# TensorE's order prefers groups of products that have been ready for some time, and the planner's durations of products and transposes are corrected: windowed attention with a rational feed-forward layer

## The chip, the cores and the metric

The kernel runs on one core of a Trainium2 chip. The metric is the device time of one execution in microseconds (us); the time of a kernel is the median of its runs.

## The reference

Attention with 8 batches, 8 heads, 576 positions and 64 values per head, in which each position looks at itself and the 63 before it, and then a feed-forward layer on the 4608 tokens (512 to 2048 to 512) with a rational function in place of an activation:

```python
scores = scale * np.matmul(q, k.transpose(0, 1, 3, 2))
mask = (rel >= 0) & (rel < window)                      # window = 64
scores = np.where(mask, scores, -1000000000.0)
scores = scores - np.max(scores, axis=-1, keepdims=True)
attn = np.exp(scores)
attn = attn / (np.sum(attn, axis=-1, keepdims=True) + 1e-09)
attn_out = np.matmul(attn, v)
...
h = x @ w_in                                            # x: 4608 x 512, w_in: 512 x 2048
P = a[0] + a[1] * h + a[2] * h2 + a[3] * h3
Q = 1.0 + np.abs(b[0]) * np.abs(h) + np.abs(b[1]) * h2
g = P / (Q + 1e-6)
return (g @ w_out).astype(np.float32)                   # w_out: 2048 x 512
```

All is float32.

## The kernel before, in words

**Tiles.** The tokens are cut into 12 chunks of 384 (`CH`), the hidden layer into 16 tiles of 128 (`NF`). One hidden tile of one chunk is a *step*. The first two chunks take their steps in halves (chunk 0 tiles 0 to 7, chunk 1 tiles 0 to 7, chunk 1 tiles 8 to 15, chunk 0 tiles 8 to 15), because the second half of the weights is still loaded and split then; from chunk 2 on, a chunk is 16 steps in a row, 192 steps in all. Each float32 matrix is split into a high and a low part (`xh` and `xl`, `wi_h` and `wi_l`, `gh` and `gl`, `wo_h` and `wo_l`), and a product is made of three.

**A step.** `ffn1` issues 12 products of 128x384 into one of two banks, `h_75` and `h_76`, by turns. ScalarE makes a square (`u`), an absolute value (`r`) and a linear form (`num`) from `h`. VectorE makes the denominator (`u<-u,b_sb,r`), and the numerator in two operations that both read `h` (`num<-num,h`, then `num<-num,ab_sb,h`): the bank is free for new products when these are done. ScalarE makes the reciprocal with a logarithm and an exponential (`r<-u`, `r<-r`); VectorE makes `gh` and, in three more operations, `gl`. Three steps later (`LAG`) `ffn2` multiplies them with the output weights: three products of 128x512 into each of the banks `o_72`, `o_73` and `o_74`, which add up over the 16 steps of a chunk. ScalarE copies them out (`ob`) at the end of it.

**A unit.** The attention of one chunk is done in four units, a pair of heads each, so that there is one unit to four steps, three steps ahead of the place where its chunk needs it (`AHEAD`). A unit is, in order: score products into `ps_s`; two VectorE operations that scale and mask them into `sm`; the row maximum (`nmx<-sm`); six exponentials on ScalarE (`sm<-sm,nmx`), which also add up the rows into `sums`; three VectorE operations in `unit_norm` (`sums<-sums`, the reciprocal `rs<-sums` and the *normalisation* `sm<-sm,rs`); six transposes of 128x128 on TensorE (`unit_transpose`), back into `ps_s`; a copy on ScalarE (`pT`); products with the values into `ps_x`, joined with the next unit's score products; and the parts `xh` and `xl` of the result, which is 128 of the 512 rows of `x` of that chunk.

**What sets the order.** The order of each engine's queue is not that of the program's text. A planner (lines 51 to 226) records every call, gives it a duration from a small table (`cost`), and then plays the program through (`plan`): again and again it takes the engine that can start first, and of the operations that are ready on it by then the one that comes first in the text; the end of that operation, plus a margin for the semaphore, is when those that depend on it become ready. The instructions are then issued in the order of the planned starts (`emit`), so that a planned time that is a little off changes the order, and nothing else: on the chip an engine takes its queue in that order and waits where an operand is missing. Groups (`pl.group`) are issued in one piece: the 12 products of an `ffn1`, the three of one output bank, the six transposes of a unit. All planned instructions carry one line in the profile, that of the call in `emit` (L226 before, L228 after).

Of the kernel before, what the change touches and what calls it, by code (L numbers as in the profile page):

```python
# [27 lines left out]
SLOTS = 3  # L28
WARM = 7
FILL = 430  # L30
C1AT = 0, 0, 1, 3
ON_PE = 2
JOIN = 4
# [17 lines left out]
class Planner:  # L51
# [58 lines left out]
    def cost(self, engine, method, out, reads, kw, args):  # L110
        if isinstance(out, Late):
            n = out.size // 4
        else:
            n = 1
            for _, k in out.ap[1:]:
                n *= k
        if engine == "SP":
            parts = 128 if isinstance(out, Late) else (out.ap[0][1] if out.tensor.__class__.__name__ != "DRamTensorHandle" else 0)
            size = mybir.dt.size(out.dtype) * n * (parts or out.ap[0][1])
            return 400, 400, size  # L120
        if engine == "PE":
            if method == "transpose":
                return 109, 270, 0
            if isinstance(args[2], Late):
                n = args[2].size // 4
            else:
                n = 1
                for _, k in args[2].ap[1:]:
                    n *= k
                if args[2].dtype == F32:  # L130
                    return (45, 270, 0) if args[1].ap[0][1] == 64 else (52, 225, 0)
            return n * 0.452, n * 0.452 + 165, 0
        if engine == "ACT":
            if "accum_out" in kw:
                return 343, 450, 0
            f = args[2] if len(args) > 2 else None
            occ = 58 + 0.813 * n
            if n == 512:
                occ = 640 if method == "copy" and getattr(out, "dtype", None) == F16 else 510
            for k in ("scale", "bias"):  # L140
                if isinstance(kw.get(k), bass.AP):
                    occ += 92
            if f in (AF.Ln, AF.Exp):
                occ += 55
            return occ, occ + 120, 0
        if engine == "DVE":
            if method == "tensor_reduce":
                n = 1
                for _, k in reads[0].ap[1:]:
                    n *= k  # L150
            if n < 16:
                return 90, 185, 0
            occ = 65 + 1.045 * n
            if isinstance(kw.get("scalar"), bass.AP):
                occ += 62
            return occ, occ + 85, 0
        if engine == "POOL":
            return (n * 2.0 + 60, n * 2.0 + 100, 0) if method in ("tensor_scalar", "tensor_copy") else (n * 2.4 + 130, n * 2.4 + 170, 0)
# [24 lines left out]
    def plan(self):  # L183
        waiting = {e: [] for e in self.free}
        missing = [len(o.before) for o in self.ops]
        for o in self.ops:
            if not o.before:
                waiting[o.engine].append(o)
        dma_free = 0
        for _ in self.ops:  # L190
            start, engine = min((max(self.free[e], min(o.ready for o in w)), e) for e, w in waiting.items() if w)
            op = min((o for o in waiting[engine] if o.ready <= start), key=lambda o: o.index)
            waiting[engine].remove(op)
            op.start, self.free[engine] = start, start + op.occ
            op.end = start + op.own + 45
            if engine == "PE":
                op.end = self.free[engine] + 200
            if engine == "SP":
                dma_free = max(dma_free, start + 750) + op.dma / (300 if start < 8000 else 390)
                op.end = dma_free + 1550  # L200
            for o in op.after:
                o.ready = max(o.ready, self.free[engine] if engine == o.engine == "SP" and self.lanes_apart(op, o) else op.end)
                missing[o.index] -= 1
                if not missing[o.index]:
                    waiting[o.engine].append(o)
# [42 lines left out]
def swa_rational_ffn(ctx: ExitStack, tc: tile.TileContext, qk, v, w_in, w_out, out):  # L248
# [107 lines left out]
    pl = Planner(nc, dict(DVE=4700, ACT=2100, PE=WARM * 430 + 1200, POOL=5000, SP=750), shares)  # L356
# [49 lines left out]
    def two_banks(c, hp, transposed):  # L406
        if c == 0 and transposed:
            return [ps_o[0], ps_o[1]], None
        if c == 0 and hp % 2:
            return [h_ring(), h_ring()], None  # L410
        return [ps_s[:, 0], ps_s[:, 1]], ps_s
# [63 lines left out]
    def unit_transpose(c, hp):  # L475
        u = live[c, hp]
        ps, both = two_banks(c, hp, True)
        with pl.group():
            for j in range(2 * PR):
                pl.tensor.transpose(ps[j // PR][:, (j % PR) * P:(j % PR + 1) * P], u["sm"][:, j, :], ident)  # L480
        pT = u["pT"] = pT_ring()
        if both is not None:
            pl.scalar.copy(out=pT, in_=both[:, :, 0:PR * P])
        else:
            for z in range(2):
                pl.scalar.copy(out=pT[:, z], in_=ps[z][:, 0:PR * P])
# [115 lines left out]
    for c, i0, i1 in phases:  # L602
        if c not in seen:
            seen.add(c)
            places += [(C1AT[k] if c == 1 else s - prev + prev // HP * k - AHEAD, c, k, s - prev if c > 1 else 0) for k in range(HP)]
        prev = i1 - i0
        s += prev
    for n, (p, c, k, free) in enumerate(places):
        joined = n >= HP + JOIN
        if joined:  # L610
            p = max(p, places[n - 1][3])
        at(p, unit_load, c, k)
        if joined:
            at(p, av_and_scores, *places[n - 1][1:3], c, k)
        else:
            at(p, unit_scores, c, k)
        at(p, unit_soft, c, k)
        at(p, unit_norm, c, k)
        at(p + 1, unit_transpose, c, k)
        if n + 1 < HP + JOIN or n + 1 == len(places):  # L620
            at(max(p + 1, free), unit_av, c, k)
# [9 lines left out]
    for k in range(HP):  # L631
        unit_scores(0, k)
        unit_soft(0, k)
        unit_norm(0, k)
        unit_transpose(0, k)
        unit_av(0, k)
# [14 lines left out]
    pl.plan()  # L651
    pl.fill("PE", ps_o[2].tensor.name, FILL, (nc.tensor.matmul, (ps_o[2], warm[:, 0:P], warm), dict(start=True, stop=True)))
    pl.emit()
# [37 lines left out]
```

## Time and profile before

| | |
|---|---|
| median of 3 runs | 982.49 us (981.6 to 982.84) |
| the profiled execution | 982.07 us, of which the span from the first to the last instruction is 980.3 |
| TensorE (PE), products / weight loads | 952.6 us (97% of the span) / 824.6 (84%) |
| VectorE (DVE) | 911.2 us (93%) |
| ScalarE (ACT) | 698.5 us (71%) |
| GpSimd (POOL) | 4.4 us (0%) |
| SyncE's transfers | 68.38 MB, 70 GB/s over the span |
| TensorE's granted clock | 0.997 of full speed |

How to read it: a busy share is a mean over stages that differ. In this kernel there are four. Up to about 150 us the weights are loaded and split while the first two chunks run; then both halves of the weights are there; from about 275 us on the chunks 2 to 11 run with one unit of attention to four steps; and at the end, from 881 us, only the last chunk's feed-forward is left. Numbers by stretch say more than the head of the page. A row of a timeline has the start and the duration in us, the engine, the operation, output and operands, and in brackets the idle time ahead of it with what ended it. The ends of TensorE's products are modelled, so a product that is shown with 0.40 us may have its successor start 0.24 us after its own start; what TensorE lost at some place is read from start to start.

### The profile page before, as it was taken

How to read it: one execution, taken by the hardware profiler on the slowest of the kernel's cores; microseconds unless marked ns; L12 is line 12 of the kernel's file. 1: busy time of each engine (PE TensorE's matmuls, PEld its weight loads, DVE VectorE, ACT ScalarE, POOL GpSimd, SP SyncE). 2: the span in 40 equal slices, each digit the busy share in tenths (PEclk: the TensorE clock that was granted, in tenths of full speed). 3: DMA queues.
4: the chain of work that ended last, by engine and by line, in shares of the span. 5: the costliest groups of instructions: out<-in, count | busy, mean ns of one | idle time of the engine just before them, and what ended most of it. 6: DMA issues, size and time to landing. Idle time of an engine off the chain costs nothing.

```text
span 980.3 us, 17701 instructions
## 1 busy us (share of the span) xinstructions
PE 952.6 (97%) x6672; PEld 824.6 (84%) x6675; DVE 911.2 (93%) x1747; ACT 698.5 (71%) x1737; POOL 4.4 (0%) x20
## 2 busy tenths in 40 slices
PE   8899999999999999999999999999999999999998
PEld 5677788888888888888888888888888888888996
DVE  6999999998999999999999999999999899999996
ACT  7988777776667667767677677667766776676664
POOL 1000000000000000000000000000000000000000
PEclk9999999999999999999999999999999999999999
DMA  9344341313103103103102200210310310300000
GB/s 360 127 171 147 122 150 39 96 50 117 51 1 117 35 17 118 35 17 116 37 17 74 79 17 26 93 51 1 118 35 17 118 35 18 100 1 2 33 1 32
DMA packets 24564, 68.38 MB, mean 70 GB/s; under 512 B 2720, under 2 KB 2720, under 8 KB 24480
## 3 DMA queue, kind: packets, MB, share of 16 engines
q1 hardware_dynamic: 24480, 67.27, 20.2%
q8 instruction: 52, 0.85, 0.4%
q14 instruction: 32, 0.26, 0.1%
HBM read 57.03 MB, written 10.22 MB: 69 GB/s over the span
## 4 chain that ended last, share of the span: by engine, by line
PE 64%; DVE 19%; ACT 10%; issue 2%; DMA 1%; ACTq 0%; DVEq 0%
PE o L226 29%; PE h L226 28%; DVE u L226 6%; PE ps_s L226 5%; ACT sm L226 4%; DVE num L226 3%; PE ps_x L226 3%; ACT r L226 2%; DVE gh L226 2%; DVE sm L226 2%; DVE nmx L226 1%; ACT u L226 1%; DVE gl L226 1%; DMA w_st<-w_out 1%; ACT num L226 1%
## 5 line engine op out<-in xcount | busy, mean ns | idle before, releaser
L226 PE MATMUL h<-xl,wi_h 128*128 128x384 f32 x768 | 260.4, 339 | 7.7 <-DVE num L226 6.2
L226 PE MATMUL h<-xh,wi_l 128*128 128x384 f32 x768 | 258.1, 336 | 0.0
L226 PE MATMUL h<-xh,wi_h 128*128 128x384 f32 x768 | 257.9, 336 | 0.0
L226 PE MATMUL o<-wo_h,gl 128*128 128x512 f32 x576 | 236.5, 411 | 2.5 <-DVE gl L226 1.7
L226 PE MATMUL o<-wo_h,gh 128*128 128x512 f32 x576 | 228.2, 396 | 0.0
L226 PE MATMUL o<-wo_l,gh 128*128 128x512 f32 x576 | 227.0, 394 | 0.0
L226 ACT ACTIVATE u<-h 128x384 f32<-128x384 f32 x192 | 94.2, 491 | 158.4 <-PE h L226 153.6
L226 PEld LDWEIGHTS h<-xl,wi_h 128*128 128x128 f32 x768 | 144.2, 188 | 20.3 <-DVE num L226 10.2
L226 PEld LDWEIGHTS h<-xh,wi_h 128*128 128x128 f32 x768 | 144.2, 188 | 7.2
L226 ACT ACTIVATE num<-h,ab_sb 128x384 f32<-128x384 f32 x192 | 129.7, 675 | 25.7 <-PE h L226 15.6
L226 PEld LDWEIGHTS h<-xh,wi_l 128*128 128x128 f32 x768 | 144.2, 188 | 0.3 <-DVE wi_l L226 0.3
L226 ACT ACTIVATE r<-u 128x384 f32<-128x384 f32 x192 | 101.3, 527 | 48.1 <-DVE u L226 44.8
L226 PEld LDWEIGHTS o<-wo_h,gl 128*128 128x128 f32 x576 | 108.1, 188 | 29.0 <-issue 5.1
L226 PEld LDWEIGHTS o<-wo_h,gh 128*128 128x128 f32 x576 | 108.5, 188 | 26.3
L226 DVE SCALAR_TENSOR_TENSOR gh<-num,ab_sb,r 128x384 fp32r<-128x384 f32 x192 | 117.9, 614 | 8.7 <-ACT r L226 1.6
L226 PEld LDWEIGHTS o<-wo_l,gh 128*128 128x128 f32 x576 | 108.7, 189 | 16.5
L226 DVE SCALAR_TENSOR_TENSOR num<-num,ab_sb,h 128x384 f32<-128x384 f32 x192 | 117.3, 611 | 5.6 <-ACT r L226 1.5
L226 DVE SCALAR_TENSOR_TENSOR u<-u,b_sb,r 128x384 f32<-128x384 f32 x192 | 117.9, 614 | 2.9 <-ACT r L226 1.0
L226 DVE SCALAR_TENSOR_TENSOR u<-num,ab_sb,u 128x384 f32<-128x384 f32 x192 | 118.1, 615 | 2.7
L226 ACT ACTIVATE r<-h,ab_sb 128x384 f32<-128x384 f32 x192 | 111.4, 580 | 11.1 <-DVE num L226 11.1
L226 DVE SCALAR_TENSOR_TENSOR u<-u,gh 128x384 f32<-128x384 f32 x192 | 106.4, 554 | 2.7
L226 DVE TENSOR_TENSOR num<-num,h 128x384 f32<-128x384 f32 x192 | 105.0, 549 | 3.5 <-ACT r L226 2.2
(74 smaller groups left out, 983.6 us busy)
## 6 DMA issues: line engine op xcount, KB each, us to landing
qk<-qk SPq DMA_DIRECT2D x44, 419.0 KB, 4.2
vt<-v SPq DMA_DIRECT2D x44, 384.0 KB, 3.6
out<-ob SPq DMA_DIRECT2D x33, 256.0 KB, 2.1
w_st<-w_out SPq DMA_DIRECT2D x15, 512.0 KB, 3.5
w_st<-w_in SPq DMA_DIRECT2D x11, 512.0 KB, 3.6
early<-qk SPq DMA_DIRECT2D x4, 419.0 KB, 5.5
early<-v SPq DMA_DIRECT2D x4, 384.0 KB, 8.1
early_wi_l<-w_in SPq DMA_DIRECT2D x3, 512.0 KB, 9.4
```

Source lines behind the costliest of these rows:

```text
L226: call(*[value(x) for x in args], **{k: value(x) for k, x in kw.items()})
```

## The change

Three edits, all in the planner's input. `MARGIN` gives TensorE 300 ns: of the operations that are ready on it, `plan` first looks among those that were ready at least 300 ns before the start, takes the first of these in the text, and only if there is none takes the first of all that are ready. A column of a product costs 0.4545 ns in place of 0.452, so a product of 384 columns 174.5 ns for 173.6, and one of 512 232.7 for 231.4. A group of six transposes holds TensorE 50 ns longer (6 x 109 + 50 = 704 for 654).

```diff
+MARGIN = dict(PE=300)
...
-            return n * 0.452, n * 0.452 + 165, 0
+            return n * 0.4545, n * 0.4545 + 165, 0
...
             start, engine = min((max(self.free[e], min(o.ready for o in w)), e) for e, w in waiting.items() if w)
-            op = min((o for o in waiting[engine] if o.ready <= start), key=lambda o: o.index)
+            able = [o for o in waiting[engine] if o.ready <= start]
+            op = min([o for o in able if o.ready <= start - MARGIN.get(engine, 0)] or able, key=lambda o: o.index)
...
     def unit_transpose(c, hp):
         u = live[c, hp]
         ps, both = two_banks(c, hp, True)
-        with pl.group():
+        with pl.group(50):
             for j in range(2 * PR):
```

No instruction is added or taken away on any engine. What changes is the order on TensorE, VectorE and ScalarE, first at about 30 us and then all through the program; SyncE's transfers keep theirs. Three places show it.

TensorE, at the transposes of a unit within a chunk, before:

```order
L226 MATMUL o_72<-wo_h_1133,gl_190 128x512
L226 MATMUL o_72<-wo_l_1146,gh_186 128x512
L226 MATMUL o_72<-wo_h_1133,gh_186 128x512
L226 MATMUL ps_s<-ident,sm_172 128x128 x6
L226 MATMUL o_73<-wo_h_1133,gl_190 128x512
L226 MATMUL o_73<-wo_l_1146,gh_186 128x512
```

and now:

```order
L228 MATMUL o_72<-wo_h_1133,gl_190 128x512
L228 MATMUL o_72<-wo_l_1146,gh_186 128x512
L228 MATMUL o_72<-wo_h_1133,gh_186 128x512
L228 MATMUL o_73<-wo_h_1133,gl_190 128x512
L228 MATMUL o_73<-wo_l_1146,gh_186 128x512
L228 MATMUL o_73<-wo_h_1133,gh_186 128x512
L228 MATMUL ps_s<-ident,sm_172 128x128 x6
```

The transposes stand behind two output banks (six products) where they stood behind one (three).

VectorE, from a unit's maximum to its normalisation and on, before:

```order
L226 TENSOR_REDUCE nmx_175<-sm_172 128x6
L226 SCALAR_TENSOR_TENSOR u_183<-num_185,ab_sb,u_183 128x384
L226 SCALAR_TENSOR_TENSOR u_182<-u_182,b_sb,r_180 128x384
L226 TENSOR_TENSOR gl_191<-u_183,r_181 128x384
L226 TENSOR_TENSOR num_184<-num_184,h_75 128x384
L226 SCALAR_TENSOR_TENSOR num_184<-num_184,ab_sb,h_75 128x384
L226 TENSOR_SCALAR sums_177<-sums_177 128x6
L226 RECIPROCAL rs_179<-sums_177 128x6
L226 TENSOR_TENSOR sm_172<-sm_172,rs_179 128x768
```

and now:

```order
L228 TENSOR_REDUCE nmx_175<-sm_172 128x6
L228 SCALAR_TENSOR_TENSOR u_183<-num_185,ab_sb,u_183 128x384
L228 SCALAR_TENSOR_TENSOR u_182<-u_182,b_sb,r_180 128x384
L228 TENSOR_TENSOR gl_191<-u_183,r_181 128x384
L228 TENSOR_SCALAR sums_177<-sums_177 128x6
L228 RECIPROCAL rs_179<-sums_177 128x6
L228 TENSOR_TENSOR sm_172<-sm_172,rs_179 128x768
L228 TENSOR_TENSOR num_184<-num_184,h_75 128x384
L228 SCALAR_TENSOR_TENSOR num_184<-num_184,ab_sb,h_75 128x384
```

The two numerator operations on `num_184`, which stood between the maximum and the operation on `sums`, stand behind the normalisation.

ScalarE in the same unit, before:

```order
L226 ACTIVATE u_182<-h_75 128x384
L226 ACTIVATE r_180<-h_75,ab_sb 128x384
L226 ACTIVATE num_184<-h_75,ab_sb 128x384
L226 ACTIVATE sm_172,sums_177<-sm_172,nmx_175 128x128 x6
L226 ACTIVATE r_180<-u_182 128x384
```

and now:

```order
L228 ACTIVATE u_182<-h_75 128x384
L228 ACTIVATE r_180<-h_75,ab_sb 128x384
L228 ACTIVATE sm_172,sums_177<-sm_172,nmx_175 128x128 x6
L228 ACTIVATE num_184<-h_75,ab_sb 128x384
L228 ACTIVATE r_180<-u_182 128x384
```

The linear form `num_184` stands behind the six exponentials, not ahead of them.

## The prediction

> **What bounds the kernel now.** I read the page's head first, then the busy times by stretch, then the waits, and last the timelines of single engines around the softmax.
>
> ```profile
> span 980.3 us, 17701 instructions
> PE 952.6 (97%) x6672; PEld 824.6 (84%) x6675; DVE 911.2 (93%) x1747; ACT 698.5 (71%) x1737; POOL 4.4 (0%) x20
> ```
>
> The head makes TensorE the bound: 97% against 93% for VectorE. By stretch (the columns are those of the first line):
>
> ```profile
> core 0: us, PE busy (x) PEld busy (x) DVE busy (x) ACT busy (x) POOL busy (x), PEclk, DMA share, GB/s
> 275.40:881.10 605.70, 601.82 (x4277) 529.02 (x4276) 565.81 (x1084) 427.06 (x1078) 0.00 (x0) 1.00 0.16 52
> 151.80:275.40 123.60, 120.48 (x930) 103.97 (x929) 115.39 (x225) 87.17 (x234) 0.00 (x0) 1.00 0.22 70
> 881.10:980.30 99.20, 94.67 (x489) 83.90 (x487) 87.41 (x157) 58.50 (x115) 0.00 (x0) 0.99 0.04 17
> 24.00:140.00 116.00, 103.78 (x704) 84.98 (x704) 115.15 (x223) 100.62 (x226) 0.00 (x0) 1.00 0.44 149
> ```
>
> From 24 to 140 us, while the weights are split, VectorE is busy 115.15 of 116 us: TensorE's order can't shorten that. From 275.4 to 881.1 us TensorE idles 3.9 us and VectorE 39.9 us. What VectorE waits for there decides (view of the waits in that stretch; us in total, times, longest):
>
> ```profile
> DVE sums L226 <- ACT sm L226: 23.1, 31, 1.2
> PE ps_s L226 <- ACT ob L226: 2.7, 4, 0.7
> PE ps_s L226 <- DVE sm L226: 1.2, 4, 0.3
> DVE gh L226 <- PE h L226: 1.5, 10, 0.2
> DVE num L226 <- ACT u L226: 1.3, 4, 0.3
> ```
>
> 23.1 us in 31 waits are for the score exponentials, which VectorE itself released by its maximum. For TensorE it waits 1.5 us in all. So over these 606 us VectorE is a second full engine: it goes round its own loop, normalisation to normalisation, and TensorE waits for it at the transposes. One such loop with its two halves, then the next (VectorE timeline):
>
> ```profile
> 314.41 0.96 DVE L226 TENSOR_TENSOR sm<-sm,rs 128x768 f32<-128x768 f32 x1
> 330.21 0.95 DVE L226 TENSOR_REDUCE nmx<-sm 128x6 f32<-128x768 f32 x1
> 332.60 0.55 DVE L226 TENSOR_TENSOR num<-num,h 128x384 f32<-128x384 f32 x1
> 333.19 0.61 DVE L226 SCALAR_TENSOR_TENSOR num<-num,ab_sb,h 128x384 f32<-128x384 f32 x1
> 334.02 0.17 DVE L226 TENSOR_SCALAR sums<-sums 128x6 f32<-128x6 f32 x1 [0.21 <-ACT sm L226]
> 334.45 0.96 DVE L226 TENSOR_TENSOR sm<-sm,rs 128x768 f32<-128x768 f32 x1
> 349.10 0.95 DVE L226 TENSOR_REDUCE nmx<-sm 128x6 f32<-128x768 f32 x1
> 352.81 0.17 DVE L226 TENSOR_SCALAR sums<-sums 128x6 f32<-128x6 f32 x1 [1.21 <-ACT sm L226]
> 353.24 0.96 DVE L226 TENSOR_TENSOR sm<-sm,rs 128x768 f32<-128x768 f32 x1
> ```
>
> The first loop takes 20.04 us (314.41 to 334.45): 15.80 to the maximum, then 4.24 in which two numerator products fill the wait, so that only 0.21 us are idle. The second takes 18.79: those two products are already done, so the maximum comes after 14.65, and then 4.14 with 1.21 us idle. The pair is 38.83 us. A third kind of loop stands at the chunk boundary:
>
> ```profile
> 294.24 0.96 DVE L226 TENSOR_TENSOR sm<-sm,rs 128x768 f32<-128x768 f32 x1
> 310.23 0.95 DVE L226 TENSOR_REDUCE nmx<-sm 128x6 f32<-128x768 f32 x1
> 295.34 0.85 PE L226 MATMUL ps_s<-ident,sm 128*128 128x128 f32 x6 [0.68 <-ACT ob L226]
> ```
>
> It takes 20.17 (294.24 to 314.41). The transposes at 295.34 start 0.14 after the normalisation ends (294.24 + 0.96), so it is that which they wait for, whatever name the row gives.
>
> The Trainium skill ("Perfetto Trace Analysis", Identifying the Most-Contended Engine) says that matmul busy time does not tell how near TensorE is to its limit, that the share of weight loads does, and that for VectorE occupancy is fair. In this stretch that is 87% (529.02 of 605.70) against 93% (565.81), so by the rule VectorE is the engine to spare. By the 99% of the matmul column the change should pay as in the second rival below; by the rule it should not. The waits above agree with the rule.
>
> **The change part by part.** The new costs, 0.4545 for 0.452 ns a column and 50 ns for a group of transposes, issue nothing; with the margin of 300 ns they only move instructions. No instruction is added or removed on any engine, and SyncE's DMAs keep their order.
>
> (1) The stretch of 31 loops from the normalisation at 275.45 to the last at 881.14.
>
> ```profile
> 275.45 0.96 DVE L226 TENSOR_TENSOR sm<-sm,rs 128x768 f32<-128x768 f32 x1
> 881.14 0.96 DVE L226 TENSOR_TENSOR sm<-sm,rs 128x768 f32<-128x768 f32 x1
> ```
>
> 605.69 us, 19.54 each. In the new order transposes stand behind six output products wherever three or six stood before, and every chunk has the same pattern: one boundary loop (VectorE's order in it is that of 294.24 to 314.41) and three loops in VectorE's order from 314.41 to its maximum. But the two numerator products that filled the wait in about half of the loops now always stand behind the normalisation, because ScalarE's `num` has moved behind the exponentials. So each of the three is 15.80 plus a wait without filling. That is 8 boundary loops and 23 others.
>
> Does 15.80 hold when TensorE is elsewhere? In the stretch VectorE's waits for TensorE are 1.5 us in 10 places; what else holds it between normalisation and maximum are its own results and ScalarE's, which wait for VectorE. So yes.
>
> The second half is 4.14 at most (349.10 to 353.24). It can be shorter, if the exponentials start as soon as the maximum ends:
>
> ```profile
> 349.90 0.58 ACT L226 ACTIVATE r<-h,ab_sb 128x384 f32<-128x384 f32 x1
> 350.36 0.40 ACT L226 ACTIVATE sm<-sm,nmx 128x128 f32<-128x128 f32 x1
> ```
>
> The maximum ends at 350.05, the first exponential starts at 350.36, behind an operation on `h_75`. With 0.05 us for the hand-over that leaves 0.26: lower bound 3.88. TensorE's `h_75` products will stand earlier against VectorE than now, since TensorE is held at the transposes, so I take a value below the middle, 3.95. A loop is then 19.75 (19.68 to 19.94).
>
> Sum: 8 x 20.17 + 23 x 19.75 = 161.4 + 454.3 = 615.6, against 605.7: **+9.9 us** (+8.3 to +14.3). As a cross-check by waits: 31 waits of 0.95 to 1.21 make 29.5 to 37.5 us in place of 23.1, +6.4 to +14.4.
>
> What TensorE gains lies inside this. Where transposes stood behind three output products they waited 0.14:
>
> ```profile
> 353.97 0.40 PE L226 MATMUL o<-wo_h,gh 128*128 128x512 f32 x1
> 354.34 0.84 PE L226 MATMUL ps_s<-ident,sm 128*128 128x128 f32 x6
> 355.26 0.40 PE L226 MATMUL o<-wo_l,gh 128*128 128x512 f32 x1
> 355.50 0.40 PE L226 MATMUL o<-wo_h,gh 128*128 128x512 f32 x1
> ```
>
> Products start 0.24 apart (355.26, 355.50), the transposes 0.37 after the product ahead. That 0.14 (normalisation at 353.24 done at 354.20) goes, and comes back at the boundary: TensorE's work ahead of those transposes is what it was, the loop ahead of them is longer. There nothing else can be issued: the next output products wait for the eviction of the chunk, and `h_75` for its bank.
>
> (2) The stretch 151.8 to 275.4. Transposes that waited for the normalisation move behind a group of `h` or output products there too (the view of waits has them with 2.0 us), and TensorE idles 3.1 us in all (123.60 - 120.48). Lower bound -3.1. Against it: the last two loops here took 35.91 (239.54 to 275.45) and are now of the kinds 18.79 and 19.75: +2.6. Between these I take **-0.5**, about the middle.
>
> ```profile
> PE ps_s L226 <- DVE sm L226: 2.0, 2, 1.0
> 239.54 0.96 DVE L226 TENSOR_TENSOR sm<-sm,rs 128x768 f32<-128x768 f32 x1
> ```
>
> (3) Up to 140 us VectorE is full and has the same instructions to do: 0. If it should find idle time there, it costs what it idles.
>
> (4) After the last normalisation TensorE alone sets the end (94.67 busy of 99.2). The last transposes now have six output products ahead of them, not three: 3 x 0.24 = **-0.7 us** left to do.
>
> Together +9.9 - 0.5 - 0.7 = +8.7 (+4.5 to +16.2). The profiled execution took 982.07 us (its span and 1.8 around it); it becomes 990.8. The median of the runs stands 0.4 above it: **991 us**, 986.6 to 998.5 if this mechanism holds.
>
> **The rivals.** *The boundary wait replaces the others and nothing else changes.* TensorE's waits at the transposes of one boundary, and of the next unit that waits long (its timeline):
>
> ```profile
> 294.33 0.34 PE L226 MATMUL h<-xh,wi_l 128*128 128x384 f32 x1
> 393.46 0.40 PE L226 MATMUL o<-wo_h,gh 128*128 128x512 f32 x1
> 394.15 0.63 PE L226 MATMUL ps_s<-ident,sm 128*128 128x128 f32 x4 [0.29 <-DVE sm L226]
> ```
>
> Against 0.17 from an `h` product to the next start (three quarters of 0.24 for its columns), 294.33 to 295.34 loses 0.84; against 0.23, 393.46 to 394.15 loses 0.46. With three of 0.14 that is 1.72 us in two chunks (156.4 us), while one boundary wait of 0.84 in each chunk is 1.68. Then the time is 982.5 - 0.5 - 0.7 = 981.3; the margin would be measured on the planner's clock and reach nothing on the chip. For it: the pattern at the boundary is the old one. Against it: VectorE's filling is gone, and its loop has no other room. 0.12.
>
> *The transposes stop waiting and TensorE is the bound*, faster. The mechanism: VectorE's 39.9 us idle in the stretch is slack, the normalisation keeps its place in time, and with six products ahead TensorE meets every one done. Price: 1.72 per 156.4 over 605.7 is 6.7, and 1.5 of the 3.1 in the stretch ahead: 982.5 - 6.7 - 1.5 - 0.7 = 973.6. It decides if a loop without filling takes under 19.3 us, which is TensorE's own work for one: (156.4 - 1.72) / 8. For it: the 97%. Against it: no loop with these operations took under 19.68 by its parts. 0.08.
>
> **How the numbers follow.** The forecast has 0.80. A measurement of this kernel tells about 0.2% (2 us) from no change. Of the 0.80 I put 0.02 within that; the first rival is at its edge and gives 0.08 to the same and 0.04 to faster; the second 0.08 to faster. Slower 0.78, same 0.10, faster 0.12. The range leaves out the second rival, most of the first and the last end of the forecast: 982.5 to 997.5.
>
> **What would show it.** VectorE's wait for the exponentials ahead of `sums` (23.1 us, 31 times in the stretch) goes to 30 to 37 with no wait of 0.2 left; loops of 19.7 to 19.9 and 20.2, four to a chunk of 79.2 to 80 us, in place of 78.2; transposes at the boundary wait 1.5 to 2 us in every chunk, and TensorE's busy time stays at 952 us while its share falls to 96%. Wrong would be: loops of 19.4 (then the fixed 15.80 was not fixed), or transposes that never wait with VectorE's idle time unchanged (the second rival).

## The result and the profile after

The changed kernel takes 989.36 us (median of 6 runs, 989.01 to 990.44), the kernel before 982.62 in the same 6 rounds (981.6 to 982.99). The ratio is 1.0072, with a 95% interval from 1.0059 to 1.0085: slower by 6.7 us. The forecast was 991, range 982.5 to 997.5.

The head of the page after shows little of it: TensorE has the same work in a longer span.

```profile
span 987.7 us, 17709 instructions
PE 952.1 (96%) x6675; PEld 828.0 (84%) x6675; DVE 909.0 (92%) x1747; ACT 700.5 (71%) x1737; POOL 4.3 (0%) x20
```

Busy times of the changed kernel from the normalisation at 275.12 to the last at 889.10 (31 loops, the same piece of work as 275.45 to 881.14 before), after it to the end, and in the stretch where the weights are split:

```profile
core 0: us, PE busy (x) PEld busy (x) DVE busy (x) ACT busy (x) POOL busy (x), PEclk, DMA share, GB/s
275.10:889.10 614.00, 601.65 (x4280) 530.86 (x4279) 565.24 (x1085) 429.28 (x1079) 0.00 (x0) 1.00 0.16 52
889.10:987.70 98.60, 94.13 (x487) 83.64 (x485) 87.57 (x156) 58.66 (x115) 0.00 (x0) 1.00 0.04 17
24.00:140.00 116.00, 104.27 (x695) 86.52 (x695) 113.03 (x219) 97.86 (x220) 0.00 (x0) 0.97 0.44 149
```

The 31 loops take 614.0 us where they took 605.7: +8.3. What lies ahead of them is 0.3 shorter (275.12 for 275.45), what lies behind them 0.6 (98.60 for 980.3 - 881.14 = 99.16). That is 7.4 us, the difference of the two profiled executions (989.50 and 982.07).

The waits in that stretch (in total, times, longest):

```profile
DVE sums L228 <- ACT sm L228: 32.0, 31, 1.2
PE ps_s L228 <- ACT ob L228: 12.3, 8, 1.6
```

VectorE's wait for the exponentials is 32.0 us in 31 waits, 23.1 before; all 31 are now full waits, none under 0.96. Its idle time in the loops grew from 39.9 to 48.8 us (614.00 - 565.24), by the same 8.9. TensorE's waits at the transposes, 3.9 us before, are 12.3, in eight places, one to a chunk. Two loops on VectorE's timeline, the boundary's and the one behind it:

```profile
294.79 0.96 DVE L228 TENSOR_TENSOR sm<-sm,rs 128x768 f32<-128x768 f32 x1
310.79 0.94 DVE L228 TENSOR_REDUCE nmx<-sm 128x6 f32<-128x768 f32 x1
314.54 0.17 DVE L228 TENSOR_SCALAR sums<-sums 128x6 f32<-128x6 f32 x1 [1.21 <-ACT sm L228]
314.97 0.96 DVE L228 TENSOR_TENSOR sm<-sm,rs 128x768 f32<-128x768 f32 x1
330.78 0.95 DVE L228 TENSOR_REDUCE nmx<-sm 128x6 f32<-128x768 f32 x1
334.22 0.17 DVE L228 TENSOR_SCALAR sums<-sums 128x6 f32<-128x6 f32 x1 [0.97 <-ACT sm L228]
334.65 0.96 DVE L228 TENSOR_TENSOR sm<-sm,rs 128x768 f32<-128x768 f32 x1
```

20.18 (16.00 and 4.18) and 19.68 (15.81 and 3.87). Every chunk has one loop of the first kind and three of the second, to a hundredth or two (one loop, of 19.73, is longer). TensorE at a boundary, 373.20 to 375.11:

```profile
373.20 0.34 PE L228 MATMUL h<-xh,wi_l 128*128 128x384 f32 x1
375.11 0.85 PE L228 MATMUL ps_s<-ident,sm 128*128 128x128 f32 x6 [1.57 <-ACT ob L228]
```

1.91 us from start to start, where two products of this kind lie 0.17 apart: 1.74 lost. At the first boundary of the stretch it is 1.54, at the others 1.73 to 1.74.

### The profile page after: what moved, and what is told of

It is laid out like the page before. It is cut to its first block, busy times and chain, and to the rows that moved or that the text cites. A ratio compares the mean times of both kernels' runs of the same rounds, so it can differ in the third digit from the quotient of the medians.

```text
span 987.7 us, 17709 instructions
## 1 busy us (share of the span) xinstructions
PE 952.1 (96%) x6675; PEld 828.0 (84%) x6675; DVE 909.0 (92%) x1747; ACT 700.5 (71%) x1737; POOL 4.3 (0%) x20
## 4 chain that ended last, share of the span: by engine, by line
DVE 42%; PE 34%; ACT 18%; issue 4%; DMA 1%; SPq 0%; ACTq 0%; DVEq 0%
PE o L228 16%; PE h L228 14%; DVE u L228 12%; DVE num L228 10%; ACT sm L228 8%; DVE gh L228 7%; ACT r L228 5%; DVE sm L228 3%; DVE gl L228 3%; DVE nmx L228 3%; PE ps_s L228 3%; ACT u L228 2%; DVE xl L228 1%; PE ps_x L228 1%; DVE w_c L228 1%
```

## The experiments

Two theories. **A, the filling**: VectorE's loop sets the pace, and the change costs time because the two numerator operations no longer fill the wait between maximum and `sums`. **B, the transposes**: they stand behind six products instead of three, come later, and hold back the unit's chain (copy, value products, scores, maximum); the order on VectorE is only a sign of it.

The table gives the median with its ratio to the kernel before of the same runs, and from the profiled execution: the time to the normalisation at which the 31 loops start, their length, what lies behind the last (to the end of the span), and VectorE's waits for the exponentials within the loops.

| kernel | median us | ratio (95%) | to the loops | 31 loops | behind | waits |
|---|---|---|---|---|---|---|
| before | 982.6 | | 275.45 | 605.69 | 99.16 | 23.1 |
| the change | 989.4 | 1.0072 (1.0059 to 1.0085) | 275.12 | 613.98 | 98.60 | 32.0 |
| margin alone | 978.2 | 0.9968 (0.9955 to 0.9980) | 272.65 | 605.18 | 98.47 | 20.6 |
| column cost alone | 987.9 | 1.0062 (1.0048 to 1.0076) | 271.84 | 614.09 | 99.17 | 32.0 |
| change without the column cost | 982.1 | 1.0005 (0.9996 to 1.0014) | 277.09 | 604.55 | 98.56 | 21.8 |
| change, filled by hand | 990.7 | 1.0095 (1.0081 to 1.0109) | 279.05 | 611.01 | 98.44 | 5.2 |
| the same, boundary transposes later | 987.3 | 1.0059 (1.0047 to 1.0072) | 279.75 | 606.40 | 98.45 | 5.3 |
| before, filling taken away by hand | 993.3 | 1.0118 (1.0103 to 1.0133) | 276.61 | 617.80 | 99.09 | 30.1 |
| change, exponential at 390 ns | 973.3 | 0.9909 (0.9896 to 0.9923) | 273.55 | 599.24 | 98.41 | 16.6 |
| the same, filling taken away by hand | 988.1 | 1.0068 (1.0055 to 1.0080) | 277.04 | 611.03 | 98.93 | 29.5 |
| change, exponential at 390 ns, without the margin | 972.5 | 0.9910 (0.9897 to 0.9924) | 272.63 | 599.60 | 98.47 | 16.6 |
| before, exponential at 390 ns | 979.0 | 0.9977 (0.9968 to 0.9986) | 276.35 | 601.83 | 98.62 | 19.0 |
| 0.449 ns, margin, exponential at 390 | 977.4 | 0.9949 (0.9935 to 0.9962) | 275.81 | 602.28 | 98.21 | 13.8 |
| margin 600, exponential at 390 | 986.6 | 1.0055 (1.0042 to 1.0067) | 277.65 | 609.37 | 96.98 | 11.9 |

Counted in the traces, the two numerator operations stand between the maximum and `sums` in 16 of the 32 units of this piece before, in none of the change and of the column cost alone, and in 16 with the margin alone and in the change without the column cost. They do so in 4 units (before) and 8 (exponential at 390 ns) where the filling was taken away by hand, in 24 in the change with the exponential at 390 ns, with and without the margin, and in the kernel before with it, and in all 32 in the two rows filled by hand and the last two of the table. From none over 16 to 24 filled units the loops get shorter (614, 605, 599 to 602 us); with all 32 filled they take 602 to 611, for reasons given below.

### The parts of the change apart

Margin alone:

```diff
 MARGIN = dict(PE=300)
-            return n * 0.4545, n * 0.4545 + 165, 0
+            return n * 0.452, n * 0.452 + 165, 0
-        with pl.group(50):
+        with pl.group():
```

> The margin of 300 ns alone, with the costs of the kernel before (0.452 ns a column, no 50 ns for the transposes). The transposes within a chunk stand behind six output products (or nine or twelve), but about half of the units keep the two numerator operations in the wait. Theory A: the mean loop stays near 19.5, and TensorE's small waits of 0.14 go: 981 to 983 us. Theory B: the transposes are as late as in the changed kernel: 987 to 990.

Column cost alone:

```diff
-MARGIN = dict(PE=300)
+MARGIN = dict(PE=0)
             return n * 0.4545, n * 0.4545 + 165, 0
-        with pl.group(50):
+        with pl.group():
```

> 0.4545 ns a column alone, no margin and no 50 ns. The transposes stand behind three output products in every unit within a chunk, but no unit has the two numerator operations in the wait. Theory A: loops of 19.67 and 20.18 as in the changed kernel, 989 to 990.5 us, and waits at the transposes behind three products of 0.3 to 0.5 us that cost nothing further. Theory B: transposes earlier than in the changed kernel, so the time of before or less: 980 to 983.

The change without its column cost:

```diff
 MARGIN = dict(PE=300)
-            return n * 0.4545, n * 0.4545 + 165, 0
+            return n * 0.452, n * 0.452 + 165, 0
         with pl.group(50):
```

> The change without its column cost (0.452 ns as before): the margin of 300 ns and the 50 ns for the transposes stay. Half of the units keep the two numerator operations in the wait. Theory A: mean loop 19.52 as with the margin alone, 977 to 981 us, so that the column cost alone carries the loss. If the 50 ns carry part of the loss: 984 us or more.

The 31 loops by busy times (columns as above) and their waits, first of the margin alone, then of the column cost alone:

```profile
272.65:877.83 605.18, 601.64 (x4280) 530.49 (x4280) 567.26 (x1087) 427.69 (x1081) 0.00 (x0) 1.00 0.16 52
```

```profile
DVE sums L228 <- ACT sm L228: 20.6, 19, 1.2
```

```profile
271.84:885.93 614.09, 604.22 (x4280) 529.18 (x4279) 565.36 (x1085) 431.69 (x1080) 0.00 (x0) 1.00 0.16 52
```

```profile
DVE sums L228 <- ACT sm L228: 32.0, 31, 1.2
PE ps_s L228 <- DVE sm L228: 2.8, 15, 0.2
```

The column cost alone brings the whole loss of the 31 loops: 614.09 against 613.98 of the change, with the same 32.0 us of waits, although its transposes stand behind three products (15 of them wait for the normalisation, 0.2 each in this view, 0.33 to 0.38 from start to start). The margin alone moves the transposes behind six or nine products within a chunk and loses nothing there: 605.18 against 605.69. Theory B is out as a cause of the +8.3. In time, taking the column cost out of the change makes it 982.1, the time of before.

Both runs with a single part left their forecast on the good side (978.2 against 981 to 983; 987.9 against 989 to 990.5), by what happens ahead of the loops: 2.8 and 3.6 us less than before; margin and 50 ns together have 1.6 more, outside the 977 to 981 that was expected. These 272 to 277 us move with the order in a way that no run here takes apart.

### The filling given back, and taken away

The planner was left as it is, and after it had set the order three operations of a unit were moved in the queues of ScalarE and VectorE, TensorE's order untouched. In the changed kernel, in 34 of 36 units:

```diff
     pl.plan()
+    pl.move_fill(True)
...
+            if into:
+                nums = [o for o in act if o.start > last.start and writes(o) == "num"][:1]
...
+            new = (first.start - 0.01, sums.start - 0.02, sums.start - 0.01) if into else (max(num.start, last.start + 0.01), norm.start + 0.01, norm.start + 0.02)
...
+                num.start, n1.start, n2.start = new
```

> The changed kernel with its TensorE order untouched. In the 34 units where it can be done, ScalarE's linear form num is issued ahead of the six exponentials instead of behind them, and VectorE's two numerator operations ahead of the operation on sums instead of behind the normalisation. Theory A (the filling of VectorE's wait is what was lost): the second half of a loop is 4.14 to 4.24 us with a wait of about 0.2 in place of 3.87 with 0.97, the first 14.65 in place of 15.80; a loop of 18.9 is under TensorE's own 19.34, TensorE becomes the bound, and 31 loops save 31 x (19.81 - 19.34) = 14.6 us against the changed kernel: 975 us, at most 980 if TensorE still loses time at the boundary. Theory B (the transposes behind six products come too late and hold back the unit's chain, the order on VectorE is only a sign of it): the first half of the loop stays at 15.8 less the two operations plus a wait for TensorE, time 988 to 990.

In the kernel before, `pl.move_fill(False)`, which moves the same three operations behind the exponentials and the normalisation in 13 units:

> The kernel before with its TensorE order untouched (transposes behind three, six and twelve products). In 13 of the 17 or so units of chunks 1 to 11 whose wait is filled, num goes behind the exponentials and the two numerator operations behind the normalisation (in four units it can't be done, since the bank would be read too late). Theory A: about 15 loops of 19.7, 8 boundary loops of 20.17 and 8 loops that still make pairs of 38.83, sum 612 in place of 605.7: 989 us. Theory B: TensorE's transposes stand where they stood, so 982.6, at most 984.

The kernel before without the filling loses 12.1 us in the 31 loops (617.80), with 30.1 us of waits. That is theory A's sign and about twice its size (+6.3 was expected). The expectation left eight loops in pairs of 38.83, but no loop of 18.79 is left: 19.87 stands in their place. The first two loops are together another 2.8 longer (41.72 for 38.96). The four loops in which only two operations are left between maximum and `sums`, with a wait of 1.5, take 19.76 as they did before. TensorE waits at the transposes too, 12.3 us in the two rows below where it waited 3.9, so this run does not show the filling alone:

```profile
DVE sums L255 <- ACT sm L255: 30.1, 31, 1.5
PE ps_s L255 <- ACT ob L255: 6.2, 4, 1.9
PE ps_s L255 <- DVE sm L255: 6.1, 7, 1.1
```

The changed kernel with the filling given back is *not* faster, 990.7 where 975 to 980 was expected. Its loops:

```profile
298.40 0.96 DVE L257 TENSOR_TENSOR sm<-sm,rs 128x768 f32<-128x768 f32 x1
318.71 0.17 DVE L257 TENSOR_SCALAR sums<-sums 128x6 f32<-128x6 f32 x1 [0.65 <-ACT sm L257]
319.14 0.96 DVE L257 TENSOR_TENSOR sm<-sm,rs 128x768 f32<-128x768 f32 x1
338.06 0.17 DVE L257 TENSOR_SCALAR sums<-sums 128x6 f32<-128x6 f32 x1
338.50 0.96 DVE L257 TENSOR_TENSOR sm<-sm,rs 128x768 f32<-128x768 f32 x1
```

Within a chunk the loop does what theory A says: 19.36 (319.14 to 338.50), no wait ahead of `sums`, TensorE's own 19.34. But the boundary's loop went from 20.18 to 20.74, so that a chunk saves only 0.4 us and the loops 3.0 in all (23 that are 0.32 shorter, 8 that are 0.56 longer). The time ahead of the loops grew by 3.9, where two units were moved too, and one of these accounts for nearly all of it:

```profile
206.29 0.55 DVE L257 TENSOR_TENSOR num<-num,h 128x384 f32<-128x384 f32 x1 [4.75 <-ACT u L257]
```

ScalarE's `num`, put ahead of this unit's exponentials, starts at 202.89 after 4.74 us of idle time for TensorE's products, and the exponentials stand behind it; VectorE then idles 4.75 us. From the normalisation ahead to this unit's is 14.95 us (192.88 to 207.83), 11.12 in the changed kernel. So a good part of the 990.7 comes from where one unit was put by hand, ahead of the loops, and not from the filling in them.

What holds the boundary is TensorE's wait at the transposes:

```profile
297.93 0.34 PE L257 MATMUL h<-xh,wi_l 128*128 128x384 f32 x1
299.50 0.85 PE L257 MATMUL ps_s<-ident,sm 128*128 128x128 f32 x6 [1.24 <-DVE sm L257]
```

1.57 from start to start, 1.40 lost, where no other unit waits. In the order of the change the boundary's transposes stand two output banks (6 x 0.235 = 1.4 us of products) nearer to those ahead of them than a regular unit's, since the banks that could go first are not copied out yet: VectorE would have to make one loop in four 1.4 us shorter than the rest. So a second cause stands beside the filling. To test it, the same kernel with these transposes put behind the first output bank of the new chunk:

```diff
+            o, late = queue[k], queue[k + 1]
+            if kind(queue[k - 1]) == "h" and kind(late).startswith("o"):
+                t = late.start + 0.01
+                if all(q.start > t for q in o.after):
+                    o.start = t
```

> The changed kernel with every unit filled by hand (990.7 us, in-chunk loops 19.35, boundary loops 20.74 with a TensorE wait of 1.40), and with the transposes of the boundary unit moved behind the first output bank of the new chunk (three products), so that TensorE's work between them and the transposes ahead is 17.9 us in place of 17.2. If the boundary wait comes from where those transposes stand: it halves, a chunk goes from 78.8 to about 78.1 us, 984 to 987. If it comes from the unit's chain on VectorE and ScalarE: 990 to 991.

```profile
298.63 0.34 PE L268 MATMUL h<-xh,wi_l 128*128 128x384 f32 x1
299.57 0.50 PE L268 MATMUL o<-wo_h,gl 128*128 128x512 f32 x1 [0.60 <-ACT ob L268]
300.37 0.82 PE L268 MATMUL ps_s<-ident,sm 128*128 128x128 f32 x6
```

TensorE now waits for the copy of the bank (0.94 from start to start, 0.77 lost) and not for the normalisation. The loops take 606.4 in place of 611.0, a chunk 78.2 in place of 78.8, the median 987.3: the saving per chunk was right, the time 0.3 above the forecast since the start was another 0.7 later. (From start to start, TensorE's work ahead of these transposes is 17.94 us without the move and 18.74 with it, not 17.2 and 17.9; the step is the one expected.) So the boundary transposes' place cost 0.6 us a chunk in this order.

### The planner's missing cost

The rows of ScalarE show what the planner had not been told. In the changed kernel, the maximum on VectorE's timeline, and then ScalarE's, with the first three of a unit's exponentials, which add up their rows:

```profile
350.46 0.94 DVE L228 TENSOR_REDUCE nmx<-sm 128x6 f32<-128x768 f32 x1
```

```profile
350.28 0.58 ACT L228 ACTIVATE r<-h,ab_sb 128x384 f32<-128x384 f32 x1
351.44 0.40 ACT L228 ACTIVATE sm<-sm,nmx 128x128 f32<-128x128 f32 x1 [0.58 <-DVE nmx L228]
351.84 0.39 ACT L228 ACTIVATE sm<-sm,nmx 128x128 f32<-128x128 f32 x1
352.22 0.39 ACT L228 ACTIVATE sm<-sm,nmx 128x128 f32<-128x128 f32 x1
```

They start 0.38 to 0.40 us apart; the planner's table has 343 ns. Corrected as well:

```diff
             if "accum_out" in kw:
-                return 343, 450, 0
+                return 390, 497, 0
```

> The changed kernel with one more cost corrected: an exponential that adds up its row is charged 390 ns of ScalarE in the planner, which is its spacing in the trace (351.84, 352.22, 352.61, ... in the changed kernel: 0.385 us), in place of 343. The planner then puts num ahead of the exponentials and the two numerator operations into the wait again, in three units of four, and the transposes go behind nine output products in two of four. Theory A: in-chunk loops of 19.35, boundary loops of 20.2, stretch 8 x 20.2 + 23 x 19.4 = 608, against 614 in the changed kernel: 981 to 985 us. Theory B (late transposes cost): the transposes are later still, 989 us or more.

```profile
273.55:872.79 599.24, 599.24 (x4281) 532.13 (x4280) 566.45 (x1087) 425.46 (x1081) 0.00 (x0) 1.00 0.16 53
```

```profile
DVE sums L228 <- ACT sm L228: 16.6, 23, 1.2
```

973.3 us, faster than before by 0.9% and better than forecast (981 to 985). In the 31 loops TensorE has no idle time that the records show: 599.24 busy in 599.24 us, 19.33 a loop, and no wait at any transposes, the boundary's included. The forecast had 20.2 for a chunk's boundary loop and 19.4 for each of its others; in fact the four loops of a chunk are 20.36, 19.34, 18.83 and 18.78 us, together 77.3, which is four times 19.33, so the boundary costs nothing extra here. The Trainium skill's rule on load share ("Perfetto Trace Analysis", Identifying the Most-Contended Engine) would still name VectorE here, 95% (566.45 of 599.24) against 89% (532.13); the measurement does not agree, since here it is TensorE that never waits.

Is it the filling, or the transposes, which now stand behind nine products in half of the units? The same kernel with `pl.move_fill(False)`, which empties two of the three filled units of a chunk and leaves TensorE's order:

> The run with the exponential at 390 ns, its TensorE order untouched. In two of the three filled units of a chunk, num goes behind the exponentials and the two numerator operations behind the normalisation. Theory A: VectorE's waits for the exponentials rise from 16.6 us in 31 loops to 30 or more, its loops go above TensorE's 19.33, 981 to 989 us. Theory B (the gain of that run came from transposes behind nine products): 973 to 976.

```profile
277.04:888.07 611.03, 605.02 (x4279) 531.54 (x4278) 565.55 (x1086) 424.62 (x1080) 0.00 (x0) 0.95 0.16 52
```

```profile
DVE sums L257 <- ACT sm L257: 29.5, 31, 1.5
PE ps_s L257 <- DVE sm L257: 4.7, 8, 0.6
```

988.1: +11.8 us in the loops with TensorE's order unchanged, the waits back at 29.5. This is the cleanest answer to A against B. And the same kernel without the margin, and the kernel before with this one cost:

```diff
-MARGIN = dict(PE=300)
+MARGIN = dict(PE=0)
```

> The changed costs and the exponential at 390 ns, without the margin. Same filling of VectorE's waits; the transposes stand behind six, nine and twelve products (one unit in four is one output bank earlier). If the costs carry the gain: 973 to 977 us. If the margin is needed for it, TensorE waits at the transposes: 979 or more.

> The kernel before with the exponential at 390 ns and nothing else. Three of four units filled, transposes behind 6, 9 and 24 products. Theory A: in-chunk loops near 19.35, boundary 20.2: 974 to 980 us. If the filling helps only together with the corrected durations of products: 981 or more.

972.5 without the margin: it isn't needed once all three costs are right. 979.0 with the old column cost: the exponential's cost alone gives 0.2%, and the same column cost that loses 0.6% alone is, with the transposes' 50 ns, worth another 0.7% beside it (972.5 against 979.0).

Two more with every unit filled. First with 0.449 ns a column and without the 50 ns for the transposes. 0.449 makes 172.4 ns of a product of 384 columns and 229.9 of one of 512; in the kernel before they start 174.6 and 233.8 ns apart on average, so this cost is further off than either of the others:

```diff
-            return n * 0.4545, n * 0.4545 + 165, 0
+            return n * 0.449, n * 0.449 + 165, 0
...
-                return 343, 450, 0
+                return 390, 497, 0
...
-        with pl.group(50):
+        with pl.group():
```

> The margin of 300 ns with a column charged 0.449 ns and an exponential 390: the planner fills every unit, with four operations of VectorE between maximum and sums in every one (three unfilled in the changed kernel, five filled), and the transposes stand behind nine output products. Theory A: sums waits of about 0.6 us in every loop and no loop above 20.2; TensorE bound within a chunk at 19.35, boundary 20.2 to 20.7: 976 to 984 us. Theory B: 989 us or more.

977.4, in the range of theory A; the waits are 0.61 us in one loop of four and 0.38 to 0.39 in the others, and no loop is above 19.91. And with a margin of 600 ns, which puts all transposes behind twelve `h` products:

```diff
-MARGIN = dict(PE=300)
+MARGIN = dict(PE=600)
...
-                return 343, 450, 0
+                return 390, 497, 0
```

> A margin of 600 ns with the changed column and transpose costs and an exponential charged 390: every unit filled, four operations in the wait, and the transposes of every unit stand behind twelve h products, so one group later than in the changed kernel. Theory A: as the run with 0.449, 976 to 984 us, unless the transposes come so late that the scores of the next unit wait for ps_s: then the first half of the loop grows above 15.8 and the time is 985 or more.

986.6, though its waits for the exponentials (11.9 us) are the lowest of the kernels with this cost. Its busy times and waits name others:

```profile
277.65:887.02 609.37, 600.79 (x4277) 531.30 (x4276) 561.08 (x1086) 428.50 (x1079) 0.00 (x0) 1.00 0.16 52
```

```profile
ACT sm L228 <- DVE nmx L228: 42.1, 31, 2.0
DVE gh L228 <- ACT r L228: 17.1, 22, 1.0
PE h L228 <- DVE num L228: 8.6, 8, 1.3
```

VectorE waits 17.1 us for ScalarE's reciprocal, and TensorE 8.6, once at each chunk's boundary, for a bank that the numerator still reads. These 8.6 us are all that TensorE idles in the loops (600.79 of 609.37 busy). Each of the eight waits ends 0.06 us after the second of the two filled numerator operations. The expectation had the scores wait for `ps_s`; the waits don't show that, and no transposes wait. So an order with every unit filled can lose what the filling gained, as TensorE waits for the bank that the filling operations read. That the late transposes bring this about, as theory B would have it, is not shown: the orders of all three engines moved together, and which of these waits comes first was not tested.

## Why the prediction was right

**The mechanism** held step by step. The loop without filling has a fixed first half of 15.80 (15.80 to 15.82 in the changed kernel but for one of 15.85, although TensorE stands elsewhere); every chunk has one loop of 20.16 to 20.18 and three of 19.67 to 19.69, with one of 19.73; the waits ahead of `sums` went to 32.0 us with none left under 0.9; the boundary's transposes wait 1.54 to 1.74 in every chunk (1.5 to 2 was foretold). The small waits of 0.14 did not all go, as it said: one unit of four still has one behind its six products. That the filling is what was lost rests on the runs: the column cost alone, with its transposes behind three products, empties all units and loses the same 8 us, and with TensorE's order unchanged the filling taken from the best kernel costs 11.8.

**The term that was mis-sized** is the second half of the loop. The prediction bounded it by 3.88 and 4.14 and took 3.95; it is 3.87, a hundredth under its lower bound, which allowed 0.05 us for the hand-over where the rows have 0.03 to 0.04. The rows show why the lower end decides: the operation on `h_75` starts before the maximum has begun (350.28) and is done by 350.86, the maximum ends at 351.40, and the first exponential starts at once (351.44). A loop is then 19.68 and not 19.75, and 23 x 0.07 = 1.6 us is the difference between the +9.9 of the sum and the +8.3 measured, and nearly all of that between 991 and 989.4. (The ends of its sum, 986.6 and 998.5, would be 987.0 and 998.7 with the 0.4 that the middle has; nothing hangs on it.)

**The stretch ahead of the loops**: -0.5 was taken, -0.3 came, and that agreement is luck. From the normalisation at 151.81 us (152.48 in the changed kernel) on, the stretch is 1.0 us shorter, not 0.5 (123.64 to 122.64). What lies ahead of that is 0.7 longer, where the prediction took nothing with VectorE full: VectorE has 113.03 us of work in 24 to 140 where it had 115.15, so it did idle there for 2 us more. The prediction named this case without a size. The parts by themselves move the time to the loops by -2.8 (margin), -3.6 (column cost) and +1.6 (margin and 50 ns), which it did not foresee. **The end**: -0.7 foretold, -0.6 measured.

**The first rival** (one boundary wait of 0.84 replaces the others) had the place and not the price: the wait is 1.74 in nearly every chunk, as the loop ahead is longer. **The second rival** (TensorE becomes the bound, 973.6) was priced on the condition that a loop gets under TensorE's 19.34. The change didn't meet it: no loop is under 19.67. In the change with the exponential's cost corrected TensorE does become the bound, at 973.3, but with the waits filled in three units of four; that this is the rival's figure is in part luck, since its price was for unfilled loops.

**What the prediction left out** is which of the three edits does it. It treated them as one order. The orders and the runs show that the column cost by itself moves ScalarE's `num` behind the exponentials and brings the loss, and that the margin costs nothing in the loops. Nor did it see that filling alone would not have been enough in this order, because of the boundary's transposes.

## What to carry to other kernels

Corrections to a planner's table of durations belong together: here correcting one duration alone moved the order to a worse one and cost 0.6%, while correcting another as well (the exponential's spacing, read from ScalarE's rows) gained 0.9%. Where two engines are both over 90% busy, read the second one's loop from one mark to the next and look at what fills its wait for a third; work that stood in that wait cost nothing here, as long as its operands were ready and no other engine waited for it, and the same work behind the wait cost time. And when an edit has parts, try each part: here they had opposite signs.

## What was not expected of the hardware

The run whose filling was taken away from the kernel with the corrected exponential was profiled at a granted TensorE clock of 0.946, 0.95 in the stretch shown above. Its 512-column products still start 0.23 to 0.24 us apart, as elsewhere, and of its five runs the two at 0.946 and 0.949 took 988.8 and 987.8 us, the three at 0.997 to 1.0 took 988.9, 987.4 and 988.1. A granted clock 5% lower cost no time that can be seen here, in a kernel whose loops (19.71 us on average) are longer than TensorE's own 19.33; why the spacing doesn't follow the clock stays open.
